# Two heads at a time in halves of the TensorE array: block-causal attention with a bilinear feed-forward, on one Trainium2 core

## The chip, the cores and the metric

The kernel runs on one core of one Trainium2 chip. Its time is the device time of one execution in microseconds (us), and the figure to be predicted is the median over several executions. Before the change three runs took 1239.2, 1240.79 and 1241.6 us, so the median is 1240.79 us.

## The reference

Eight batches of eight heads, 576 positions, 64 numbers a head. Attention is block-causal in blocks of 64 positions, and its output (4608 tokens of 512 numbers) goes into a bilinear feed-forward with 1536 hidden columns:

```python
scores = scale * np.matmul(q, k.transpose(0, 1, 3, 2))
mask = block_i >= block_j          # blocks of 64 positions
scores = np.where(mask, scores, -1000000000.0)
attn = np.exp(scores - np.max(scores, axis=-1, keepdims=True))
attn = attn / (np.sum(attn, axis=-1, keepdims=True) + 1e-09)
x = np.matmul(attn, v)             # then heads side by side: (4608, 512)
out = ((x @ w_a) * (x @ w_b)) @ w_out
```

All inputs are float32. q and k are drawn about four times larger than in the plain problem, so the scores need more than one low-precision product.

## The kernel before

Much of the kernel's arithmetic is done on float32 numbers that are split in two: a high part in the format float32r (fp32r), which TensorE takes in one pass, and the rest, the low part, also in fp32r. A plain float32 matmul is used where nothing is split; it shows in the trace as two records of one matmul.

There are three stages. The first is attention, head by head, with the first third of the feed-forward (four of the twelve blocks of 128 hidden columns, called the MoE below) filled in between. The second finishes that first third, and the third does the other eight blocks by another scheme. The change touches the first stage alone.

One head in the first stage, by the names of the code:

- `softmax` makes the scores. Positions are taken in four query tiles of 128 (t = 0 to 3, with 192, 320, 448 and 512 keys) and one "side" tile of 128 by 128 for the 64 positions that are left over at each end. TensorE (PE) writes the scores to a PSUM bank (tile `s`, or `sl` for t = 3), VectorE (DVE) sets the masked corner with a memset and takes the row maximum (`top`, a TENSOR_REDUCE to `nm`; `nb` joins the maxima of t = 3 and side), and ScalarE (ACT) computes the exponential with the sum of each row (`exps`, an ACTIVATE and a READ_ACCUMULATOR, to tile `e`). DVE makes the reciprocal `rc` of the sums, and GpSimd (POOL) multiplies `e` by it, tile by tile.
- `turn` transposes `e` on PE in blocks of 128 by 128 (fourteen for a head, into the PSUM tile `tp`, of which there are two). ACT copies `tp` to `ah` in fp32r, and DVE writes the low part to `al`.
- `values` multiplies by v. v too is split, and its high and low parts stand side by side as 128 columns (`v2`), so that one matmul gives both products; `ah` and `al` are run through it one after the other, and ACT and DVE add the two halves of the result to `xf` (`avlo`). ACT and POOL split `xf` for the MoE (`xh`, `xl`).

Scores are two fp32r products with 128 contraction rows. To that end `split_q` and `split_k` make the high and low parts for a pair of heads, and `spread` copies them by DMA, issued from SyncE's queue (SP), so that 64 rows of one head hold the high and 64 the low part of q against the same part of k. The first eight heads (`NATIVE = 8`) use plain float32 for scores and output; each then uses 64 of PE's rows for scores and 64 of its columns for the output.

The order of the work is a table, `SLOT`: for a slot s, one head long, it lists which step of which head comes next and how many units of filling follow it. `want` turns the place in the slots into a count of MoE matmuls that should have been emitted by then; they start in slot 10 (`MOE_FROM = 10.2`). `PE_ORDER` is empty, so a scheduler then settles the order of the instructions on each engine. `mm3` (line 223) makes the MoE's matmuls, twelve to a PSUM bank (tiles `ps` and `pso`), and there are two such banks: before the next but one group of twelve starts, ACT must have copied the bank out (`a`, line 247, or `ob`, line 560), or DVE must have multiplied it (`hf`, line 249). Weights arrive packed and are converted on DVE and ACT (`convert_w`) during the first ten slots.

## Time and profile before

| | before |
|---|---|
| time, median of three runs | 1240.79 us (1239.2 to 1241.6) |
| span of the profiled execution | 1238.6 us |
| PE busy, share of the span | 1222.5 us, 99% |
| DVE, ACT, POOL busy | 974.6, 706.6, 415.5 us |
| mean granted TensorE clock | 0.994 |
| first matmul of the MoE | 95.2 us |
| last matmul of `values` | 628.4 us |

The span runs from the first to the last instruction of the profiled execution; its own time is not listed apart, and the three timed runs lie 0.6 to 3.0 us above the span, their median 2.2 us. "Busy" is the time in which an engine had at least one instruction at work. Matmuls overlap one another, and so do instructions of ACT and DVE by about 0.1 us, so what an instruction costs a full queue is the distance from its start to the next one's start, not its own duration.

### The profile page before, as it was taken

The numbers are of one execution on the slowest core, as the hardware profiler recorded it, in microseconds if no ns is written. First come the engines' busy times: TensorE is split into PE (matmuls) and PEld (weight loads), VectorE is DVE, ScalarE is ACT, GpSimd is POOL, SyncE is SP. The second block draws the span as 40 slices with busy tenths as digits, with TensorE's granted clock in tenths as the row PEclk, the third lists the DMA queues.
The fourth block names the chain that finished last, engine by engine and source line by source line (L and its number), as shares of the span: only waits on it lengthen the run. The fifth ranks groups of instructions, "written<-read, shape, count | busy, mean of one in ns | idle before, by whom it ended". The sixth has DMA issues, their size and how long they took to land.

```text
span 1238.6 us, 23305 instructions
## 1 busy us (share of the span) xinstructions
PE 1222.5 (99%) x7849; PEld 1170.0 (94%) x7849; DVE 974.6 (79%) x2485; ACT 706.6 (57%) x1770; POOL 415.5 (34%) x583
## 2 busy tenths in 40 slices
PE   9989999999999999999999999999999999999998
PEld 5668999999999999999999999999999999999998
DVE  6898888777877778778889988878878677677654
ACT  5788878788788887888756345334334222222210
POOL 4467666566665666656500022022021000000000
PEclk8999999999999999999999999999999999999999
DMA  6468766767667776676234266266298344144131
GB/s 222 140 185 224 199 161 166 188 170 185 164 172 181 176 185 164 169 182 158 71 121 150 92 152 167 82 157 162 76 258 272 122 141 127 40 140 126 28 103 64
DMA packets 86583, 187.13 MB, mean 151 GB/s; under 512 B 11200, under 2 KB 46016, under 8 KB 86464
## 3 DMA queue, kind: packets, MB, share of 16 engines
q1 hardware_dynamic: 74944, 166.76, 48.6%
q0 software_dynamic: 6912, 9.44, 4.8%
q10 hardware_dynamic: 4608, 9.44, 2.2%
q8 instruction: 63, 1.03, 0.3%
q14 instruction: 56, 0.46, 0.1%
HBM read 87.03 MB, written 47.19 MB: 108 GB/s over the span
## 4 chain that ended last, share of the span: by engine, by line
PE 85%; DVE 7%; DMA 3%; ACT 2%; issue 1%; POOL 1%; SPq 0%; ACTq 0%; DVEq 0%; POOLq 0%
PE pso_z L792 15%; PE ps L223 12%; PE psx_z L746 8%; PE psw_z L746 8%; PE psv_z L746 8%; PE tp L474 8%; PE pso L223 5%; PE s L398 5%; PE psy_z L746 4%; PE av L523 3%; PE av L529 3%; PE sl L398 2%; PE av L513 2%; PE s L418 1%; DMA kp<-kT 1%
## 5 line engine op out<-in xcount | busy, mean ns | idle before, releaser
L223 PE MATMUL ps<-xh,wab 128*128 128x288 f32 x1024 | 240.7, 303 | 0.0
L792 PE MATMUL pso_z<-h_z,wo 128*128 128x384 f32 x1152 | 203.1, 334 | 0.0
L451 POOL TENSOR_SCALAR e<-e,rc 128x512 f32<-128x512 f32 (+3 forms) x256 | 154.6, 616 | 137.7 <-DVE rc L448 122.7
L792 PEld LDWEIGHTS pso_z<-h_z,wo 128*128 128x128 f32 x1152 | 199.9, 188 | 0.4 <-ACT h_z L112 0.3
L223 PEld LDWEIGHTS ps<-xh,wab 128*128 128x128 f32 x1024 | 172.0, 188 | 3.4
L223 PE MATMUL ps<-xl,wab 128*128 128x288 f32 x512 | 154.2, 301 | 0.0
L478 DVE TENSOR_TENSOR al<-tp,ah 128x512 fp32r<-128x512 f32 x224 | 131.7, 607 | 27.7 <-ACT ah L476 26.7
L112 ACT CAST h_z<-u_z 128x384 fp32r<-128x384 f32 x96 | 49.3, 514 | 180.0 <-DVE u_z L771 163.4
L476 ACT CAST ah<-tp 128x512 fp32r<-128x512 f32 x224 | 116.7, 533 | 53.0 <-PE tp L474 49.5
L474 PE MATMUL tp<-ident,e 128*128 128x128 f32 x832 | 135.9, 278 | 5.0 <-DVE al L478 1.8
L855 POOL DMA_DIRECT2D part<-pt x48 | 42.8, 1012 | 291.4 <-ACT pt L854 291.3
L474 PEld LDWEIGHTS tp<-ident,e 128*128 128x128 f32 x832 | 100.5, 141 | 20.0 <-issue 6.7
L223 PE MATMUL pso<-hh,wo 128*128 128x288 f32 x480 | 118.6, 308 | 0.0
L746 PE MATMUL psx_z<-xh,wab 128*128 128x384 f32 x384 | 116.4, 338 | 1.8 <-DVE u_z L764 1.8
L407 ACT ACTIVATE e<-s,nm 128x192 f32<-128x192 f32 (+2 forms) x192 | 101.8, 530 | 28.3 <-DVE nm L404 18.4
L746 PE MATMUL psw_z<-xh,wab 128*128 128x384 f32 x384 | 116.2, 338 | 0.0
L746 PE MATMUL psv_z<-xh,wab 128*128 128x384 f32 x384 | 116.2, 338 | 0.0
L404 DVE TENSOR_REDUCE nm<-s 128x1 f32<-128x128 f32 (+3 forms) x256 | 109.8, 430 | 2.1
L223 PEld LDWEIGHTS ps<-xl,wab 128*128 128x128 f32 x512 | 96.4, 188 | 3.6 <-POOL xl L115 0.2
L398 PE MATMUL s<-k,q 128*128 128x256 f32 x336 | 80.7, 321 | 2.1 <-ACT e_s L407 1.6
L223 PEld LDWEIGHTS pso<-hh,wo 128*128 128x128 f32 x480 | 81.5, 189 | 1.2
L115 POOL TENSOR_TENSOR v<-vr,v 128x320 fp32r<-128x320 f32 x56 | 49.7, 887 | 91.6 <-ACT v L112 78.6
(147 smaller groups left out, 2857.9 us busy)
## 6 DMA issues: line engine op xcount, KB each, us to landing
k<-kp SPq DMA_DIRECT2D x112, 288.0 KB, 4.2
xr<-xd SPq DMA_DIRECT2D x48, 384.0 KB, 4.0
q<-qp SPq DMA_DIRECT2D x112, 160.0 KB, 2.5
raww<-wab SPq DMA_DIRECT2D x24, 512.0 KB, 3.8
qp<-qT SPq DMA_DIRECT2D x32, 320.0 KB, 3.2
vr<-vm SPq DMA_DIRECT2D x64, 160.0 KB, 3.3
kp<-kT SPq DMA_DIRECT2D x32, 288.0 KB, 3.3
xd<-xf ACTq DMA_DIRECT2D x32, 288.0 KB, 4.8
```

The lines of the kernel that those rows point to most:

```text
L112: nc.scalar.copy(hi, src)
L115: return lo_eng.tensor_tensor(lo, src, f32(hi), op=ALU.subtract)
L223: mm = nc.tensor.matmul(ps, w_, d_, start=(i == 0), stop=(i == n - 1))
L398: mark = nc.tensor.matmul(ps[:, :w], qm[:, q0[t]:q0[t] + P], kk[:, :w], start=(i == 0), stop=(i == len(ks) - 1))
L404: nc.vector.tensor_reduce(nm[:, t:t + 1], view, axis=AX.X, op=ALU.max, negate=True)
L407: nc.scalar.activation(out, view, AF.Exp, bias=bias, accum_out=sm[:, t, :1])
L451: nc.gpsimd.tensor_scalar(ev, ev, rc[:, t:t + 1], 1.0, op0=ALU.mult, op1=ALU.mult)
L474: mark = nc.tensor.transpose(tp[:, c], src, ident)
L476: nc.scalar.copy(ah[:, :m, cols], tp[:, :m])
L478: return nc.vector.tensor_tensor(al[:, :m, cols], tp[:, :m], f32(ah[:, :m, cols]), op=ALU.subtract)
L746: nc.tensor.matmul(ps, wt[:, i, iw], j[:, ix], start=start and kp == 0 and i == 0 and j is xh, stop=kp == KP - 1 and i == 1, skip_group_ch ...
L792: nc.tensor.matmul(ps, wt[:, a, osl], b, start=i == 0, stop=i == 3 * len(fs) - 1)
```

## The change

The unit of the first stage becomes a pair of heads, h = 0 and 1.

- Scores (`softmax`): q and k of the pair lie under each other in 128 partitions, as they are loaded. Head 0 uses PE's rows 0 to 63 and head 1 rows 64 to 127, matmul by matmul in turn, each into a PSUM bank of its own (`ps_sc` has 4 banks, before 3). There are three fp32r products for each tile (high by high, high by low, low by high). The tiles of a pair come in two steps: t = 3, side and t = 1 in the first, t = 2 and t = 0 in the second. Narrow tiles are no longer widened to 256 columns.
- Output (`values`): plain float32 for every head. v and the transposed weights `ah` are not split: no `al`, no `split_v`, no `avlo`. Head 0 writes the columns' lower half (PSUM partitions 0 to 63) and head 1 the upper half of one tile `av`, in turn, and DVE copies the tile to `xf` in two instructions. `av` takes its bank from the two `tp` tiles.
- `spread` and its DMAs go. The split of q and k for a pair stays.
- The transposes are the same, but t = 0 of both heads shares one `tp` and one copy.
- `NATIVE = 6` now counts pairs, so twelve heads have plain float32 scores. The matmuls that kept the clock up in the first two slots (`KEEP`) go. Four buffers of `e` instead of two.
- `SLOT` is now for a pair, and `PE_ORDER = ["PE"]`: PE takes its instructions in the order in which the code emits them; the other engines are ordered by the scheduler as before.

The core of the diff:

```diff
-PE_ORDER = []
-NATIVE = 8
+PE_ORDER = ["PE"]
+KEEP = {}
+NATIVE = 6
...
-    ps_sc = psum(right, "ps_sc", 3)
+    ps_sc = psum(right, "ps_sc", 4)
...
-    def spread(i):
-    def split_v(i):
...
+    rows = slice(D), slice(D, P)
+    def products(p, x, y):
+        if p < NATIVE:
+            return [(x[:, 0], y[:, 0])]
+        x, y = x.bitcast(F32R), y.bitcast(F32R)
+        return [(x[:, 1], y[:, 1]), (x[:, 1], y[:, 0]), (x[:, 0], y[:, 1])]
...
+        def scores(t, outs):
+            for j, (qq, kk) in enumerate(qk):
+                for h, r in enumerate(rows):
+                    keys = ends(kk[r]) if t == NT else kk[r, :nk[t]]
+                    mark = nc.tensor.matmul(
+                        outs[h], qq[r, q0[t]:q0[t] + P], keys, start=j == 0, stop=j == len(qk) - 1)
...
+        def both(out, c, src, cols, start, stop):
+            for i, r in enumerate(rows):
+                mark = nc.tensor.matmul(
+                    out[r], v[:, i, c], a[:, i, src, cols], start=start, stop=stop, skip_group_check=True)
+        for c in range(NCH):
+            a0 = max(P * c - BLK, 0)
+            both(av[:, a0:], c, c, slice(a0, W), c == 0, False)
+        both(av[:, W - BLK:], NCH, SIDE, SC[1], False, True)
+        mark = both(av0, NCH, SIDE, SC[0], True, True)
+        nc.vector.tensor_copy(xf[:, BLK:], av)
+        nc.vector.tensor_copy(xf[:, :BLK], av0)
...
+    SLOT = [(V_, -2, 0), (S_, 0, 12), (T_, -1, 7), (T_, -1, 7), (T_, -1, 8), (S_, 0, 12), (T_, -1, 6),
+            (T_, -1, 6), (T_, -1, 6), (T_, -1, 8)]
```

How the change moves the instructions is seen at two places, in the middle of the stage (batch 3, head 4). The first is PE at the start of that head's scores. A row gives line, operation, output, inputs and columns. In the program before, the names are `s1` (t = 1 and side), `sl` (t = 3), `ps0` (a MoE group of twelve), `k2` and `q2` (the spread parts):

```order
L223 MATMUL pso_1_1_3_3945<-hh_1_1_3_3677,wo3_85 128x288
L418 MATMUL s13_4_3981<-k23_4_3768,q23_4_3767 128x128 x2
L398 MATMUL sl3_4_3980<-k23_4_3768,q23_4_3767 128x512 x2
L223 MATMUL ps0_2_0_1_3997<-xh2_0_0_2651,wab1_80 128x288
L223 MATMUL ps0_2_0_1_3997<-xl2_0_0_2652,wab1_80 128x288
```

The same place after the change, where `s33_4_0` and `s33_4_1` are t = 3 of the two heads and `av0` the last tile of an earlier pair's output:

```order
L471 MATMUL av03_0_3270<-ah3_0_3092,v3_0_2758 64x64 x2
L383 MATMUL s33_4_0_3300<-k3_4_2918,q3_4_2921 128x512
L383 MATMUL s33_4_1_3301<-k3_4_2918,q3_4_2921 128x512
L383 MATMUL s33_4_0_3300<-k3_4_2918,q3_4_2921 128x512
L383 MATMUL s33_4_1_3301<-k3_4_2918,q3_4_2921 128x512
L383 MATMUL s33_4_0_3300<-k3_4_2918,q3_4_2921 128x512
L383 MATMUL s33_4_1_3301<-k3_4_2918,q3_4_2921 128x512
L383 MATMUL s13_4_0_3302<-k3_4_2918,q3_4_2921 128x128
```

Two matmuls for one head between MoE matmuls became six for two heads, directly behind the output of the pair before the last; two more tiles of six follow before the next MoE matmul.

The second place is ACT, where the exponentials of that head stand among the copies out of the MoE's banks. Before (`e0_...` from `s1`, `sl`, `s0` are the head's exponentials, `a` the copy of a MoE bank, `ah` of a transposed tile):

```order
L407 ACTIVATE e0_s_115,sm0_113<-s13_4_3981,nb3_4_3979 128x128
L407 ACTIVATE e0_3_109,sm0_113<-sl3_4_3980,nb3_4_3979 128x512
L407 ACTIVATE e0_0_106,sm0_113<-s03_4_4022,nm3_4_3977 128x192
L247 COPY a_2_0_1_4039<-ps0_2_0_1_3997 128x288
L476 CAST ah3_3_4056<-tp3_3_3_4058 128x4x128
L407 ACTIVATE e0_1_107,sm0_113<-s13_4_3981,nm3_4_3977 128x320
```

After the change, from the pair's first exponential (t = 3, side, then further on t = 2 and t = 0 of both heads; `q4_0` is the high part of q of a later pair):

```order
L391 ACTIVATE e0_3_109,sm0_138<-s33_4_0_3300,nb3_4_3299 128x512
L391 ACTIVATE e1_3_117,sm0_138<-s33_4_1_3301,nb3_4_3299 128x512
L391 ACTIVATE e0_s_113,sm0_138<-s13_4_0_3302,nb3_4_3299 128x128
L391 ACTIVATE e1_s_121,sm0_138<-s13_4_1_3303,nb3_4_3299 128x128
L456 COPY ah3_2_3358<-tp3_2_3_0_3359 128x4x128
L247 COPY a_2_0_1_3365<-ps0_2_0_1_3345 128x288
```

```order
L391 ACTIVATE e0_2_108,sm0_138<-s23_4_0_3409,nm3_4_3297 128x448
L391 ACTIVATE e1_2_116,sm0_138<-s23_4_1_3410,nm3_4_3297 128x448
L348 ACTIVATE q4_0_3457<-qr4_0_3458 128x640
L391 ACTIVATE e0_0_106,sm0_138<-s03_4_0_3411,nm3_4_3297 128x192
L391 ACTIVATE e1_0_114,sm0_138<-s03_4_1_3412,nm3_4_3297 128x192
L247 COPY a_2_0_2_3462<-ps0_2_0_2_3392 128x288
L112 CAST k4_0_3454<-kr4_0_3455 128x576
```

Each copy `a` of a MoE bank now stands behind four exponentials and one more instruction, where before two or three exponentials stood between two copies.

More of the change, by code (lines that the diff above doesn't have):

```diff
@@ L283, in attention_then_bilinear_ffn @@
     NCH = (S - BLK) // P
-    c0 = [min(max(P * c - BLK, 0), S - BLK - 256) for c in range(NCH)]
     W = S - BLK
@@ L313, in attention_then_bilinear_ffn, with pair_of @@
     xs_all = {}
[L315 to L317 removed]
+    def pair_of(p):
         b, h = divmod(2 * p, H)
[L320 to L331 removed]
@@ new lines, in load_qk, with load_v, parts_of @@
+    def load_qk(p):
+        b, h, n = pair_of(p)
+        take(p, "k", S, kT[b, h:h + 2].rearrange("h d s -> (h d) s"))
+        take(p, "q", SQ, qT[b, h:h + 2].rearrange("h d s -> (h d) s"))
+    def load_v(p):
+        b, h, n = pair_of(p)
+        vv = heads[p]["v"] = apool.tile([P, 2, NCH + 1, D], F32, tag="v", name=f"v{n}", bufs=3)
+        for j in range(2):
+            nc.sync.dma_start(vv[:, j], vm[b, h + j])
+    def parts_of(p, tag):
+        return heads[p].pop(f"{tag}r"), *(heads[p][tag].bitcast(F32R)[:, j] for j in (1, 0))
@@ L663, in attention_then_bilinear_ffn @@
             due += m
-            now = s + due / fill
+            now = 2 * (s + due / fill)
             while n_conv < 5 * int(now * CONV_PER_SLOT + CONV0):
```

343 lines of the change are left out of this document (121 added, 222 removed).

## Prediction

> **What bounds the kernel now.** I read the page first, then the windows, then the order of time on PE, ACT and DVE inside one stretch of the attention stage. A change smaller than 0.2% (2.5 us) could not be told from none.
>
> From the page: the span, and the busy time of PE and of its weight loads.
>
> ```profile
> span 1238.6 us, 23305 instructions
> PE 1222.5 (99%) x7849; PEld 1170.0 (94%) x7849; DVE 974.6 (79%) x2485; ACT 706.6 (57%) x1770; POOL 415.5 (34%) x583
> ```
>
> Next the windows: length, then busy time and count by engine. The first row is the start, the second the middle of the stage. The third holds the `sl` matmuls alone (two to a head), the fourth the MoE matmuls of line 223, from head 10's scores to head 62's.
>
> ```profile
> 5.00:94.60 89.60, 83.57 (x500) 56.74 (x498) 78.01 (x225) 67.85 (x185) 47.31 (x56) 0.92 0.59 180
> 267.10:577.80 310.70, 310.30 (x2243) 298.20 (x2242) 247.03 (x785) 250.46 (x706) 191.03 (x273) 1.00 0.69 173
> 94.60:596.80 502.20, 35.17 (x104) 1.00 0.71 177
> 94.60:596.80 502.20, 337.04 (x1824) 1.00 0.71 177
> ```
>
> In the middle PE is busy 310.30 of 310.70 us: the stage is as long as PE's work, and DVE, ACT and POOL have room. 104 records are 52 heads in 502.2 us, 9.66 us a head or **19.32 us a pair**, and 1824 / 26 = 70 MoE matmuls go with each pair. So the price of the change is the difference per pair, times 26, with the start apart.
>
> What PE spends is read from starts (start, length, engine, line, matmul, count). Rows that no difference needs are left out, among them the second record of line 527 and the four of line 529 behind the first row.
>
> ```profile
> 301.71 0.22 PE L527 MATMUL av<-ah,v 128*128 128x128 f32 x1
> 302.63 0.29 PE L223 MATMUL pso<-hh,wo 128*128 128x288 f32 x1
> ...
> 303.03 0.56 PE L398 MATMUL s<-k,q 128*128 128x448 f32 x2
> 303.43 0.30 PE L223 MATMUL pso<-hh,wo 128*128 128x288 f32 x1
> ...
> 304.54 0.43 PE L223 MATMUL pso<-hh,wo 128*128 128x288 f32 x2
> 304.80 0.30 PE L223 MATMUL pso<-hl,wo 128*128 128x288 f32 x1
> 304.94 0.49 PE L474 MATMUL tp<-ident,e 128*128 128x128 f32 x3
> ...
> 305.64 0.29 PE L223 MATMUL pso<-hl,wo 128*128 128x288 f32 x1
> ...
> 305.91 0.34 PE L418 MATMUL s<-k,q 128*128 128x128 f32 x2
> 306.08 0.68 PE L398 MATMUL sl<-k,q 128*128 128x512 f32 x2
> 306.60 0.29 PE L223 MATMUL ps<-xh,wab 128*128 128x288 f32 x1
> ...
> 309.10 0.96 PE L523 MATMUL av<-ah,v 128*128 128x512 f32 x4
> 309.90 0.46 PE L398 MATMUL s<-k,q 128*128 128x320 f32 x2
> 310.19 0.43 PE L223 MATMUL ps<-xh,wab 128*128 128x288 f32 x2
> ```
>
> A MoE matmul takes (304.94 - 304.54) / 3 = 0.133 us. Between 304.94 and 305.64 lie four transposes and two MoE matmuls: (0.70 - 0.27) / 4 = 0.108 us a transpose. Score matmuls: 0.26 us for 512 columns, 0.20 for 448, 0.145 for 320, 0.085 for 128; for 256 columns I interpolate 0.12. A head's scores are twice their sum, 1.62 us; its output 0.92 + 0.80 = 1.72 us; its 14 transposes 1.51 us. A pair is then 2 x 4.85 + 70 x 0.133 = 19.0 us, near the 19.32 that the windows give.
>
> **The change, part by part.** *Row halves.* Do two heads in two halves of the rows run side by side? Before, odd and even float32 heads stand in different halves, and where they meet the trace shows it:
>
> ```profile
> 32.15 0.37 PE L418 MATMUL s<-kp,qp 64*128 64x128 f32 x1
> 32.15 0.69 PE L398 MATMUL sl<-kp,qp 64*128 64x512 f32 x1
> 32.36 0.27 PE L418 MATMUL s<-kp,qp 64*128 64x128 f32 x1
> 32.69 0.59 PE L398 MATMUL sl<-kp,qp 64*128 64x512 f32 x1
> ```
>
> Both start at 32.15. So a pair's scores cost one head's three products: 3 x (0.23 + 0.20 + 0.145 + 0.11 + 0.11) = **2.39 us** (0.23 for a second 512-column matmul, whose weights are loaded in time; 0.11 for 192 and 128 columns, a little above the measured 128). Before they cost 3.24. Without overlap they would cost 4.78.
>
> *Column halves, and the price of going from one form to another.* Float32 output with 64 columns, and what stands around it:
>
> ```profile
> 36.31 0.66 PE L474 MATMUL tp<-ident,e 128*128 128x128 f32 x4
> 36.90 1.32 PE L513 MATMUL av<-ah,vr 128*64 128x128 f32 x12
> 38.15 0.80 PE L398 MATMUL s<-kp,qp 64*128 64x320 f32 x2
> 38.88 0.45 PE L513 MATMUL av<-ah,vr 128*64 128x64 f32 x4
> ```
>
> Four transposes take 0.59 us to the next start instead of 0.43, so 0.15 us goes into the new form. The next twelve records (eight of 128 columns and four of 64, 1280 columns) take 1.25 us, 1.10 without such a step: 0.86 ns a column and record, two records a matmul. The 320 columns take 0.73 us, 0.19 more than 2 x 320 x 0.86 ns. So each change of form costs 0.15 to 0.2 us, and before there are none in the middle of the stage, where all rows say 128*128.
> Now one head's output is 512 + 448 + 320 + 192 + 64 + 64 = 1600 columns, 2.75 us in float32. If the two heads overlap, a pair costs **2.75 us**, against 3.44 before; if not, 5.50. No row of before has two column halves at work, so both ends stay in the range; I take 2.75, since row halves, the nearest rows, overlap fully. The Trainium skill ("TensorEngine Tiling (Array Packing)", Key Properties) says that different tiles load and multiply in parallel, which no run here shows for columns.
>
> There are five changes of form a pair (into the output, from it to the scores, out of the scores, and once more into and out): 0.9 us. The three DMA queues and POOL lose work or keep it (no `spread`, no `v` split; POOL scales q of the float32 pairs, which DVE did), and PE waited for none of it. DVE loses `al` and `avlo`, ACT `avlo`: they were hidden behind PE and gain nothing by themselves.
>
> PE's work is 70 x 0.133 + 28 x 0.108 + 2.39 + 2.75 + 0.9 = **18.4 us**, 0.9 below 19.32.
>
> *New waits.* PE now keeps to the written order, and there are two MoE banks. PE can't begin the next but one group of twelve before ACT has copied the bank. Ahead of these copies stand now the exponentials of a pair. ACT's starts, DVE's maxima, and the mean of a 448-column maximum by form:
>
> ```profile
> 302.63 0.74 ACT L343 ACTIVATE qp<-qp 128x640 fp32r<-128x640 f32 x1
> 303.27 0.57 ACT L536 COPY avlo<-av 64x512 f32<-64x512 f32 x1
> ...
> 305.76 0.64 ACT L407 ACTIVATE e<-s,nm 128x448 f32<-128x448 f32 x1
> ...
> 306.39 1.07 ACT L476 CAST ah<-tp 128x512 fp32r<-128x512 f32 x2
> 307.33 0.42 ACT L560 COPY ob<-pso 128x288 f32<-128x288 f32 x1
> ...
> 308.94 0.37 ACT L407 ACTIVATE e_s<-s,nb 128x128 f32<-128x128 f32 x1
> ...
> 309.30 0.69 ACT L407 ACTIVATE e<-sl,nb 128x512 f32<-128x512 f32 x1
> ...
> 309.96 0.43 ACT L407 ACTIVATE e<-s,nm 128x192 f32<-128x192 f32 x1
> ...
> 310.36 0.41 ACT L247 COPY a<-ps 128x288 f32<-128x288 f32 x1
> ```
>
> ```profile
> 306.79 0.69 DVE L404 TENSOR_REDUCE nm<-sl 128x1 f32<-128x512 f32 x1 [0.15 <-PE sl L398]
> ...
> 308.00 0.28 DVE L404 TENSOR_REDUCE nm<-s 128x1 f32<-128x128 f32 x1
> ```
>
> ```profile
> L404 DVE TENSOR_REDUCE nm<-s 128x1 f32<-128x448 f32 x64 | 39.2, 613 | 0.6
> ```
>
> By starts an exponential with its sum takes 0.36 us (128 columns), 0.40 (192), 0.63 (448), 0.66 (512); a copy to `ah` 0.47; q's high part 0.64.
> The second step of the scores: from the start of the last t = 2 product it ends after about 0.4; a memset (put at 0.1) and the first maximum (0.61) bring it to 1.1; then 2 x 0.63 + 0.64 + 2 x 0.40 on ACT and 0.41 for the copy: done at 4.2. PE in the meantime does 0.20 + 3 x 0.11 (t = 0), 0.2 (form), 12 matmuls, four transposes and 2 more matmuls: 0.73 + 14 x 0.133 + 0.43 = 3.0. **It waits 1.2 us.**
> The first step: end of t = 3 at 0.4, two maxima 1.3 (0.69 the second, a little less the first), four memsets and the side's two maxima 0.9 (0.28 a maximum; the memsets are my estimate), `nb` 0.3 (an estimate too, two tiny instructions): 2.9; then 2 x 0.66 + 2 x 0.36 + 0.47 + 0.41 = 2.9: copied at 5.8. PE: 0.23 + 3 x (0.11 + 0.145) + 0.2 + 24 x 0.133 + 8 x 0.108 = 5.3. **It waits 0.5 us.**
>
> A pair takes 18.4 + 1.7 = 20.1 us, 0.8 more than 19.32; 26 pairs make **+21 us**. These chains are the weakest terms; each may be 0.5 us off, and so the sum 26 us either way.
>
> *The start.* Until 94.6 us DVE is busy 78.0 of 89.6 us (scores and weights), and the change leaves both there. Less PE work can gain 12 us at most; but within a slot output, scores and transposes now follow one another in written order, two heads at a time, with DVE between them. I take nothing, with 10 us each way. What follows attention is unchanged.
>
> Sum against the profiled execution: 1238.6 + 21 = 1260 us of span. The median lies 2.2 us above it, hence **1262 us**.
>
> **The rivals.**
> 1. *The waits don't come*: if ACT is ahead of these sums, PE's 18.4 us stand alone, 26 x 0.9 = 23 us less: 1217 us. For it: ACT is busy 250 of 311 us, with less to do afterwards. Against: what counts is not its load but what stands ahead of the copy. It decides from waits under 0.9 us a pair.
> 2. *Both effects cancel*: 1240 us.
> 3. *Halves overlap in part*, say three quarters of the saving: (2.39 + 2.75) / 4 = 1.3 us a pair more, 1296 us. Against: the second `sl` record above starts 0.54 us after the first; 512 x 0.86 ns is 0.44, and the rest a change of form, so nothing is lost there. The Trainium skill ("TensorE: Matmul & The Clock Gate", Part 3: Packing small matmuls) reports 2.38 times for three column tiles and 3.07 for four row tiles, 0.79 and 0.77 of the ideal; an estimate by that page is 1.4 us a pair more, 1299 us.
> 4. *Column halves don't overlap*: 2.75 us a pair more, 1262 + 72 = 1334 us. For it: nothing shows that they do.
> 5. *Row halves don't overlap in fp32r* (the rows above are float32): 2.4 us more, less the first wait, which PE would then fill: 1.9 x 26 = 49, 1311 us.
>
> **How the numbers follow.** My forecast has a chance of 0.45 (1236 to 1288 us by the chains and the start), the first rival 0.30, the second 0.06, the third 0.07, the fourth 0.09, the fifth 0.03. The range goes from 1204 (most of the first rival, with some gain at the start) to 1308; outside stay the fourth and fifth and what is left of the first, 0.19 in all. Faster 0.30, no change 0.06, slower 0.64.
>
> **What would show it.** Score records of one pair in `64*128` with two starts within 0.02 us, and `128*64` records of `av` likewise, would show the overlap; 19.3 or 20.1 us between the scores of neighbouring pairs decides between first rival and forecast; PE's idle time in front of line 223, put down to ACT's `a` and `ob`, should be 1.7 us a pair. I am wrong if that idle time is under 0.9 us, or if the pair's output takes 5.5 us.

## The result: slower by 4.7%

The changed kernel takes 1298.70 us (1296.1 to 1300.42, four runs) against 1241.19 us (1239.2 to 1242.09) for the kernel before beside it: 1.0469 times as long, 95% interval 1.0447 to 1.0490, or 57.5 us more. The forecast was 1262 us: the sign is right, the size is not.

### The profile page after: what moved, and what is told of

It is laid out like the page before. It is cut to its first block, busy times and chain, and to the rows that moved or that the text cites. A ratio compares the mean times of both kernels' runs of the same rounds, so it can differ in the third digit from the quotient of the medians.

```text
span 1298.6 us, 22050 instructions
## 1 busy us (share of the span) xinstructions
PE 1208.5 (93%) x8045; PEld 1098.4 (85%) x8045; DVE 790.7 (61%) x1932; ACT 620.6 (48%) x1550; POOL 351.9 (27%) x540
## 4 chain that ended last, share of the span: by engine, by line
PE 74%; DVE 11%; ACT 11%; issue 3%; DMA 1%; SPq 0%; ACTq 0%; DVEq 0%
PE pso_z L722 14%; PE ps L223 9%; PE psw_z L676 7%; PE psx_z L676 7%; PE av L471 7%; PE pso L223 7%; PE psv_z L676 7%; PE s L383 6%; ACT e L391 6%; PE tp L453 5%; DVE nm L388 4%; PE psy_z L676 3%; ACT ah L456 2%; ACT e_s L391 1%; ACT a L247 1%
## 5 line engine op out<-in xcount | busy, mean ns | idle before, releaser
L223 PE MATMUL ps<-xh,wab 128*128 128x288 f32 x1024 | 230.4, 304 | 18.0 <-ACT a L247 18.0
L434 POOL TENSOR_SCALAR e<-e,rc 128x512 f32<-128x512 f32 (+3 forms) x256 | 149.2, 602 | 129.5 <-DVE rc L430 127.8
L456 ACT COPY ah<-tp 128x512 f32<-128x512 f32 x224 | 134.3, 604 | 40.0 <-PE tp L453 40.0
L388 DVE TENSOR_REDUCE nm<-s 128x1 f32<-128x512 f32 (+4 forms) x320 | 146.8, 484 | 10.3 <-PE s L383 6.3
L383 PE MATMUL s<-k,q 64*128 64x512 f32 (+3 forms) x900 | 113.1, 369 | 26.2 <-ACT e L391 25.8
L223 PE MATMUL pso<-hh,wo 128*128 128x288 f32 x480 | 106.1, 302 | 20.9 <-ACT ob L502 13.0
L383 PEld LDWEIGHTS s<-k,q 64*128 64x128 f32 x900 | 78.7, 193 | 52.4 <-ACT e L391 37.2
L453 PEld LDWEIGHTS tp<-ident,e 128*128 128x128 f32 x832 | 105.3, 146 | 18.7 <-issue 8.9
L391 ACT ACTIVATE e<-s,nm 128x448 f32<-128x448 f32 (+2 forms) x192 | 102.5, 540 | 38.2 <-DVE nm L388 37.9
L480 DVE COPY xf<-av 128x512 f32<-128x512 f32 x32 | 22.1, 691 | 138.7 <-PE av L471 138.1
L471 PE MATMUL av<-ah,v 128*64 128x64 f32 (+4 forms) x768 | 99.4, 410 | 3.0 <-ACT ah L456 3.0
```

The lines of the kernel that those rows point to most:

```text
L223: mm = nc.tensor.matmul(ps, w_, d_, start=(i == 0), stop=(i == n - 1))
L383: mark = nc.tensor.matmul(outs[h], qq[r, q0[t]:q0[t] + P], keys, start=j == 0, stop=j == len(qk) - 1)
L388: nc.vector.tensor_reduce(nm[:, h, t:t + 1], view, axis=AX.X, op=ALU.max, negate=True)
L391: nc.scalar.activation(out, view, AF.Exp, bias=bias, accum_out=sm[:, h, t, :1])
L434: nc.gpsimd.tensor_scalar(ev, ev, rc[:, h, t:t + 1], 1.0, op0=ALU.mult, op1=ALU.mult)
L453: mark = nc.tensor.transpose(tp[:, c], src, ident)
```

## The profile after

First the page of the changed kernel: the span, and the busy time of PE and the other engines.

```profile
span 1298.6 us, 22050 instructions
PE 1208.5 (93%) x8045; PEld 1098.4 (85%) x8045; DVE 790.7 (61%) x1932; ACT 620.6 (48%) x1550; POOL 351.9 (27%) x540
```

Every engine has less to do than before, PE by 14 us, and still the span is 60 us longer: PE now waits. Where it waits, the windows say (length, busy time and count by engine, granted clock, DMA share, GB/s): the start up to the first MoE matmul, nine pairs in the middle, all from the first MoE matmul to the first of stage 3, and stage 3.

```profile
5.00:114.90 109.90, 75.98 (x322) 42.43 (x320) 79.66 (x208) 60.69 (x162) 46.16 (x64) 0.66 0.41 130
311.51:500.30 188.79, 172.59 (x1389) 148.88 (x1388) 80.25 (x270) 115.81 (x333) 87.42 (x138) 1.00 0.25 75
114.90:728.20 613.30, 569.16 (x4550) 496.60 (x4549) 280.75 (x901) 374.90 (x1057) 260.72 (x408) 1.00 0.25 76
728.20:1298.60 570.40, 559.80 (x3170) 556.54 (x3169) 429.76 (x825) 183.57 (x331) 42.60 (x48) 0.99 0.46 130
```

The last two stretches of the kernel before, by the same marks (its first MoE matmul starts at 95.2 us):

```profile
94.60:677.00 582.40, 579.21 (x4177) 555.63 (x4176) 474.27 (x1459) 455.81 (x1258) 324.07 (x465) 1.00 0.66 167
677.00:1238.60 561.60, 556.22 (x3170) 554.77 (x3168) 421.61 (x803) 181.47 (x327) 42.77 (x48) 1.00 0.45 129
```

By the exact starts (first MoE matmul 114.92 us, before 95.23; first matmul of stage 3 at 728.27, before 677.04) the 60.0 us fall into three parts: **19.7 in the start**, 613.35 - 581.81 = **31.5 from there to stage 3**, and 570.3 - 561.6 = **8.7 in stage 3**.

Next, one pair on PE in order of time (start, length, matmul, count, and in brackets the idle time before it with what ended it). The last two rows are the output's first matmuls one pair and nine pairs later.

```profile
311.51 2.92 PE L471 MATMUL av<-ah,v 128*64 128x512 f32 x24
314.37 1.74 PE L383 MATMUL s<-k,q 64*128 64x512 f32 x18
...
320.07 0.29 PE L223 MATMUL ps<-xh,wab 128*128 128x288 f32 x1
321.00 0.40 PE L223 MATMUL pso<-hh,wo 128*128 128x288 f32 x1 [0.65 <-ACT a L247]
...
322.95 1.18 PE L383 MATMUL s<-k,q 64*128 64x448 f32 x12
...
326.31 0.30 PE L223 MATMUL pso<-hh,wo 128*128 128x288 f32 x1
327.81 0.40 PE L223 MATMUL pso<-hh,wo 128*128 128x288 f32 x1 [1.21 <-ACT ob L502]
...
332.49 0.65 PE L471 MATMUL av<-ah,v 128*64 128x512 f32 x2
...
500.26 0.65 PE L471 MATMUL av<-ah,v 128*64 128x512 f32 x2
```

The pair's output takes 314.37 - 311.51 = 2.86 us, its two score steps 1.67 and 1.11 us (to the next matmul), changes of form included: both kinds of halves overlap fully. A pair takes (500.26 - 311.51) / 9 = 20.97 us. Twice PE stops for a MoE bank: the starts lie 0.93 and 1.50 us apart where neighbours lie 0.13 apart. With the slower first matmul after each stop (the next one starts 0.24 us later, not 0.13) that is 0.9 + 1.5 = 2.4 us a pair. The profile's own account of PE's waits in the nine pairs (us, times, longest) counts only the idle time and has 16.2 us, 1.8 a pair, all of it for the copies `a` and `ob`:

```profile
PE ps L223 <- ACT a L247: 7.0, 8, 1.2
PE pso L223 <- ACT ob L502: 6.0, 5, 1.2
PE pso L223 <- ACT a L247: 3.2, 5, 0.7
```

ACT and DVE show why:

```profile
318.03 0.69 ACT L391 ACTIVATE e<-s,nb 128x512 f32<-128x512 f32 x1 [2.04 <-DVE nb L412]
...
319.71 0.37 ACT L391 ACTIVATE e_s<-s,nb 128x128 f32<-128x128 f32 x1
...
320.52 0.43 ACT L247 COPY a<-ps 128x288 f32<-128x288 f32 x1
...
324.70 0.63 ACT L391 ACTIVATE e<-s,nm 128x448 f32<-128x448 f32 x1 [1.43 <-DVE nm L388]
...
325.94 0.73 ACT L348 ACTIVATE q<-qr 128x640 fp32r<-128x640 f32 x1
...
326.96 0.42 ACT L391 ACTIVATE e<-s,nm 128x192 f32<-128x192 f32 x1
...
327.35 0.41 ACT L502 COPY ob<-pso 128x288 f32<-128x288 f32 x1
```

```profile
314.37 0.69 DVE L480 COPY xf<-av 128x512 f32<-128x512 f32 x1 [2.23 <-PE av L471]
...
315.37 1.29 DVE L388 TENSOR_REDUCE nm<-s 128x1 f32<-128x512 f32 x2 [0.18 <-PE s L383]
...
319.90 0.11 DVE L395 MEMSET s<- 64x64 f32 x1 [1.97 <-ACT e_s L391]
```

The two copies stand behind four exponentials and a copy `ah`, and behind five activations, as the prediction had it, and its chains were only a little short. They count from the start of the last t = 3 product, which the trace has at 314.94 us: the first maximum starts 0.43 us later (forecast 0.4), the exponentials 3.1 us later (2.9), and the copy `a` ends 6.0 us later (5.8). PE comes to the matmul that needs the bank after 5.3 us, as forecast. In the second step `ob` ends 4.3 us behind the start of the last t = 2 product (4.2). DVE's copy of the output, which stands ahead of the maxima, doesn't delay them: DVE waits for the scores behind it. The last row shows DVE idle for 1.97 us: the memset of the t = 1 tile waits for ACT's exponentials of the side block, whose columns lie in the same bank.

In the start PE waits for something else. The largest row of PE's waits up to the first MoE matmul, changed kernel first and then the kernel before (us, times, longest):

```profile
PE s L383 <- ACT e L391: 25.1, 10, 11.6
```

```profile
PE s L398 <- ACT e_s L407: 2.4, 3, 1.3
```

Both score steps of a pair use all four score banks, so the second step waits until the first step's exponentials have emptied them, and there is no MoE work yet to put beside it. The longest wait is the first pair's, and DVE's first instructions tell its cause: the weights' first conversion waits for its DMA, and the first maximum stands behind it (in e2 below, without that, it runs at 7.34 us).

```profile
9.66 0.43 DVE L141 TENSOR_SCALAR sw<-raww 128x512 int32<-128x512 int32 x1 [8.26 <-DMA raww<-wab]
...
12.85 0.68 DVE L388 TENSOR_REDUCE nm<-s 128x1 f32<-128x512 f32 x1
```

In the first 35 us of stage 3 PE waits, longest (2.1 and 1.6 us) for DVE's tile `u_z`. These 35 us, changed kernel first and then the kernel before: DVE is as busy, but PE gets through 155 matmuls instead of 197, and the granted clock is 0.90 instead of 1.00.

```profile
728.20:763.20 35.00, 30.45 (x155) 28.53 (x155) 33.84 (x75) 14.37 (x27) 0.00 (x0) 0.90 0.43 137
```

```profile
677.00:712.00 35.00, 34.16 (x197) 33.84 (x196) 33.99 (x71) 15.15 (x29) 0.00 (x0) 1.00 0.35 110
```

By counts of starts the loss appears between the 80th and the 140th matmul of the stage (the 80th starts 0.7 us earlier after the stage's first than before the change, the 140th 7.1 us later, the last 8.7 us later); DVE converts weights in that time. How much of the loss is the wait and how much the clock behind it isn't separated. When the last transpose of attention starts, 1959 of the 2256 MoE matmuls of line 223 have started, and 1919 before: 40 fewer are left to convert beside.

How the loss builds up, counted from the starts in four traces. A cell gives the start of the last transpose of that pair and, by then, the MoE matmuls started; "lag" is the difference to the kernel before, less 0.133 us for each MoE matmul in hand. The last two columns belong to experiments below (e1 and c4).

| pair | before | changed | lag | e1, lag | c4, lag |
|---|---|---|---|---|---|
| 1 | 33.4 / 0 | 43.3 / 0 | 9.9 | 9.8 | 3.5 |
| 4 | 86.2 / 0 | 106.8 / 0 | 20.6 | 19.6 | 4.9 |
| 6 | 124.0 / 88 | 146.6 / 110 | 19.7 | 18.6 | 4.7 |
| 9 | 180.1 / 278 | 205.8 / 304 | 22.2 | 19.5 | 4.2 |
| 20 | 394.4 / 1071 | 436.1 / 1096 | 38.4 | 19.4 | -2.3 |
| 30 | 588.4 / 1791 | 644.3 / 1816 | 52.6 | 19.4 | -7.8 |

Half of the start's loss is there after the first pair, all of it after the fourth. From the ninth pair on 1.5 us come with every pair.

## The experiments

The theory (A): the loss has three places, the MoE banks whose copies stand behind exponentials in ACT's program, the start's score banks with the first conversion ahead of the first maximum, and stage 3's late weights. Rivals: B, the pair is bound by its own round from scores to exponentials, or by DVE; C, the low granted clock costs the start; D, a gain in the start is given back, because the weight conversions bound it; E, the halves' order in PE's program doesn't matter. All kernels start from the changed one. The times are medians, the ratios are to the kernel before in the same comparison.

### The waits at the MoE banks

**e1**: `a` and `ob` are copied by DVE.

```diff
-nc.scalar.copy(a_sb, ps[:, :n])
+nc.vector.tensor_copy(a_sb, ps[:, :n])
...
-nc.scalar.copy(ob, ps)
+nc.vector.tensor_copy(ob, ps)
```

> The copies a and ob, which empty the MoE banks, are on DVE instead of ACT. Theory A (of the 57.5 us lost, the larger part are two waits of PE in each pair for a MoE bank whose copy stands behind exponentials in ACT's queue, 0.9 and 1.47 us where the pair's length is 20.97): the idle time ahead of the MoE matmuls falls from 39 us to under 8, neighbouring pairs lie 18.6 to 18.9 us apart, the time is 1242 to 1256 us. Rival B (the pair's length is set by the round from scores through maxima and exponentials back to the score banks, or by DVE once it has the copies too): the wait moves to the scores, pairs stay 20.2 us or more apart, the time is 1280 to 1299 us.

Measured: 1268.41 us, ratio 1.022 (1.0195 to 1.0246), 30 us less than the change. All waits of PE in ten pairs (301.55 to 496.1 us, 19.45 us each):

```profile
PE tp L453 <- ACT ah L456: 4.0, 18, 0.3
```

No wait for a MoE bank is left, and that is worth 30 us, net of the waits that took their place. For 19.45 us a pair is not 18.6: transposes now wait for their two banks, whose copies `ah` stand behind the same exponentials. Neither A nor B had the number, and A's place was right.

**e9** was meant for stage 3: `behind = 3 * F1 * NO + 40` leaves 40 more MoE matmuls behind attention.

> 40 MoE matmuls fewer are put beside attention and 40 more are left behind it, as many as before the change. Theory A (stage 3 lasts 8.7 us longer because DVE has 40 matmuls less time to convert the next weights in, so that PE waits between the 80th and the 140th matmul of the stage): the stage lasts 561 to 564 us instead of 570.3, the attention ends some 5 us earlier and the stretch behind it is 5 us longer, the time is 1290 to 1294 us. Rival (DVE's order in that stretch and not its length): 1297 to 1300 us.

Measured: 1273.82 us, ratio 1.0274 (1.0256 to 1.0291). Stage 3 takes 565.7 us, 4.6 less; but most of the gain of 25 us is elsewhere: pairs lie 19.8 us apart (300.0 to 498.1 us, ten pairs), although copies and engines are untouched. PE's waits in that stretch, and two rows of ACT in one pair:

```profile
PE tp L453 <- ACT ah L456: 5.0, 15, 0.6
PE ps L223 <- ACT ob L502: 1.0, 5, 0.2
```

```profile
404.67 0.40 ACT L502 COPY ob<-pso 128x288 f32<-128x288 f32 x1 [0.94 <-PE pso L223]
405.78 0.69 ACT L391 ACTIVATE e<-s,nb 128x512 f32<-128x512 f32 x1 [0.71 <-DVE nb L412]
```

A bank takes 12 matmuls and a pair 72, so the banks end at the same places in every pair. In the changed kernel one ends with the 12th matmul behind the first score step, just as the exponentials begin (318.03 us above), and its copy comes behind them at 320.52, although ACT had been idle for 2.04 us. 40 matmuls later in the count a bank ends with the fourth, and its copy fits into that idle time. Two runs test this reading; the expectations speak of 24 matmuls a bank, which is the pair of banks that one block of hidden columns takes. 48 keeps the phase by either count.

**e11** and **e12**: 48 and 32 instead of 40.

> 48 MoE matmuls, twice a bank's 24, are put behind attention instead of 40. Phase theory (what took 1.2 us a pair off with 40 was that the bank changes fell elsewhere in the pair, 40 being 16 more than 24): the pairs lie 20.9 to 21.0 us apart again, only stage 3 gains its 4.6 us or a little more, the time is 1291 to 1296 us. Rival (fewer MoE matmuls beside attention help by themselves): 19.7 to 19.9 us, 1270 to 1276 us.

> 32 MoE matmuls behind attention: the bank changes come 8 matmuls later in the pair than in the changed kernel. Phase theory: the distance between pairs differs from both 20.97 and 19.79 us, anywhere from 19.2 to 21.5 us, and the waits stand at other MoE runs than the two of the changed kernel. Rival (fewer MoE matmuls beside attention help by themselves): 19.7 to 20.0 us and 1273 to 1278 us, with the waits at the same places.

Measured: e11 1298.82 us (1.0469, 1.0436 to 1.0501) with pairs 20.97 us apart again; e12, one run, 1289.34 us with pairs 20.4 us apart, and its waits at other places (from 306 to 493 us 7.1 us ahead of transposes and 2.6 ahead of MoE matmuls). The phase decides, not the amount. And e11 gained nothing although its stage 3 takes only 564.4 us: the 48 matmuls (6.4 us) went from a stretch that waits anyway to one in which PE has to do them.

### The start

**e2**: `CONV0 = 0`, and each step of a conversion is ordered behind the latest pair's `rc` on DVE.

```diff
-            if paced:
-                behind_of(ins, "hf")
+            behind_of(ins, "hf" if paced else "rc")
```

> The first weight conversion stands behind the first pair's softmax on DVE, and each later one behind the latest pair's rc. Theory A (the start's 19.7 us are lost before the first transpose, at 31.1 us where it was 16.3 us, most of it because the first maximum stands behind a conversion that waits for the weights): the first maximum runs at about 7 us where it was 12.9, the first transpose at 24 to 26 us, the first MoE matmul at 107 to 110 us where it was 114.9, the time is 1290 to 1294 us. Rival C (the low granted clock of the start, 0.50 to 0.84, costs it): the first transpose comes at 29 us or later, the time is 1297 to 1300 us. Rival D (a conversion that starts later keeps the first MoE matmul where it is): the first transpose comes earlier and the first MoE matmul does not.

Measured: 1299.51 us (1.0469, 1.0445 to 1.0493). The first maximum runs at 7.34 us instead of 12.85:

```profile
7.34 1.29 DVE L386 TENSOR_REDUCE nm<-s 128x1 f32<-128x512 f32 x2 [5.93 <-PE s L381]
```

The first transpose starts at 21.05 us instead of 31.06 and the first MoE matmul at 108.7 instead of 114.9; the sixth pair ends at 146.1 us instead of 146.6. A's cause is right for the first pair. The total went as D says, gained and given back before the sixth pair, but D's reason isn't shown. From the first MoE matmul to the sixth pair's end DVE is busy 26.1 us (16.0 in the change), PE waits 3.2 us there for one `ah`, and behind that wait the granted clock is 0.58 for four us (136.6 to 140.6), where the change has 1.00 in these pairs.

**e3**: 108 matmuls of zeros (`KEEP`), into an idle MoE bank, in the first five pairs.

> Matmuls of zeros into an unused MoE bank stand in the first five pairs' program on PE, 106 in all, to keep the clock granted. Rival C (the low clock costs the start): granted clock 0.9 to 1.0 from 20 to 120 us, the first MoE matmul 8 to 11 us earlier than 114.9 us, the time 1288 to 1291 us. Theory A (the first pair's wait for DVE costs it, and from the first av matmul on the two kernels need the same 70.4 us to the first MoE matmul, although the clocks differ): the clock rises, the first MoE matmul comes 0 to 4 us earlier, the time is 1295 to 1300 us.

Measured: 1299.42 us (1.0466, 1.0438 to 1.0494). The granted clock up to the first MoE matmul rises from 0.66 to 0.87, and that matmul starts at 113.4 us, 1.5 earlier. But the zeros are work too: PE is busy 88.7 us up to there, against 76.0, so this run alone can't price the clock. What speaks against C as the main cost is c4 below, whose first MoE matmul starts 18.2 us earlier than the change's at a granted clock of 0.70.

**e8**: in the first five pairs the t = 2 scores use the two MoE banks, which are idle then.

```diff
-            return [ps_sc.tile([P, 512], F32, tag="sc", name=f"s{t}{n}_{h}") for h in range(2)]
+            pl, tag = (ps_mm, "mm") if t == 2 and p < 5 else (ps_sc, "sc")
+            return [pl.tile([P, 512], F32, tag=tag, name=f"s{t}{n}_{h}") for h in range(2)]
```

> In the first five pairs, before any MoE matmul, the second step's larger tile uses the two idle MoE banks for its scores. Theory A (the start is lost because both score steps share four banks, so that the second step's scores wait for the first step's exponentials, 25 us in the first 108 us): that wait falls under 12 us, the first MoE matmul comes at 103 to 108 us instead of 114.9, and the gain is kept: 1287 to 1293 us. Rival D (the start is bounded by the weight conversions on DVE and by the pairs' own chains, as in the run where the conversions came later): the first MoE matmul comes earlier by less than 3 us or the gain is given back by pair 5, 1296 to 1300 us.

Measured: 1294.91 us (1.0466, 1.0437 to 1.0495, so not told apart from the change). PE's two largest waits up to 104.2 us:

```profile
PE tp L454 <- ACT ah L457: 15.8, 9, 3.8
PE s L384 <- ACT e L392: 11.6, 3, 10.8
```

The score banks' waits are gone but for the first pair's, and a wait of the transposes has taken their place. Still the first MoE matmul starts at 104.3 us, 10.6 earlier; at the sixth pair's end 6.1 us of it are left. The stretch between the two, e8 first and then the change:

```profile
104.20:140.50 36.30, 33.43 (x230) 28.28 (x229) 18.41 (x61) 24.20 (x69) 15.73 (x22) 0.91 0.29 93
114.90:146.60 31.70, 29.44 (x231) 25.42 (x229) 15.95 (x58) 23.43 (x68) 13.78 (x21) 1.00 0.23 69
```

With the same matmuls PE is busy 4.0 us longer, at a lower clock: 0.50 from 112.2 to 116.2 us and 0.68 in the next four, right behind a wait for score banks. So most of what is given back here goes with the clock. No run holds the clock in that place.

**e6**: the maxima of the t = 1 tile come before the side block's exponentials, so that DVE does not wait for ACT (`[0]` stands for memset and maximum, `[1]` for the exponential).

```diff
+        masked(1, ps[1], [0])
         for h in range(2):
             exps(LAST, h, eb[h][0][LAST], ps[LAST][h], nb[:, h, :1])
...
-        masked(1, ps[1])
+        masked(1, ps[1], [1])
```

> Only the order of the softmax is changed: the maxima of the tile that shares its bank with the side block come before the exponentials of that block, so that DVE does not wait for ACT in the first step (it waited 1.5 to 2 us there in each pair). Theory A (the start is the round from scores through maxima and exponentials back to the four score banks): PE's wait for score banks before 107 us falls from 25 us to 13 to 18 us, the 28 transposes of the fourth pair end at 97 to 101 us instead of 106.8, and 7 to 10 us of it are kept to the sixth pair. In the steady stretch all six exponentials now stand in one piece ahead of the copy a, so the first step's wait for a MoE bank grows from 0.9 to 1.2 to 1.8 us and takes 5 to 15 us back: 1290 to 1303 us. Rival (the start is bounded by the weight conversions): the sixth pair ends within 3 us of where it did, 1297 to 1312 us.

Measured: 1324.52 us (1.0686, 1.0669 to 1.0703), 26 us more than the change. The start did as A has it (fourth pair 6.5 us earlier, though only 2.9 of them are left at the sixth). The rest is the other side: six exponentials now stand in one piece ahead of `a`, and pairs lie 22.06 us apart. PE's waits in nine pairs:

```profile
PE ps L223 <- ACT a L247: 14.2, 10, 1.7
PE pso L223 <- ACT a L247: 6.9, 4, 1.7
PE pso L223 <- ACT ob L506: 4.8, 4, 1.2
```

A shorter chain for the scores is a longer one for the copies behind it; I had priced that at 5 to 15 us, and it was about 28 (from the sixth pair's end to the last one's 560.4 us, in the change 532.8).

### Stage 3

**e7**: `STEP = 680` instead of 800, so the conversions behind attention come faster.

> The weight conversions after attention come every 680 instead of every 800 units of MoE work. Theory A (the 8.7 us lost in stage 3 are PE's wait for weights there, because 40 MoE matmuls fewer are left after attention to convert beside): stage 3 lasts 563 to 567 us instead of 570.3, the time is 1290 to 1296 us. Rival (DVE has no room for them there): 1297 to 1301 us.

Measured: 1296.34 us (1.0463, 1.0447 to 1.0478). Stage 3 takes 568.4 us, 1.9 less, and the total is not told apart from the change. That is little: in runs that leave this stage as it is it takes from 569.0 (e8) to 572.2 us (e3). At the stage's 140th matmul the loss has fallen from 7.1 to 2.4 us, but at the 400th it is 6.7 (8.1 in the change), so it moved more than it went. Only e9 (565.7 us) and e11 (564.4 us) lie clearly below: the stage is shorter when more MoE matmuls are left in front of it. That DVE's time for the conversions is the reason is argued and not shown, and in e11 the total gained nothing by it.

### The halves

**e5**: all of the first head's output products, then all of the second's. **e10**: three of one, three of the other. **e4**: scores of a tile, three products of one head, then three of the other. The edit of e4:

```diff
-            for j, (qq, kk) in enumerate(qk):
-                for h, r in enumerate(rows):
+            for h, r in enumerate(rows):
+                for j, (qq, kk) in enumerate(qk):
```

> In the output all 12 products of the first head are issued, then all 12 of the second, instead of in turns. If two column halves run beside each other only when neighbours in PE's order (theory A, which reads 2.86 us for the 24 records as full overlap): the 24 records take 5.4 to 5.7 us, a pair 2.6 us more, the time is 1298.7 + 2.6 x 30 = 1365 to 1385 us. Rival E (PE lets the second head's records run ahead of the first's by themselves): 2.9 us for the 24 records, 1297 to 1302 us.

> The output's products are issued three of the first head, three of the second, and so on. The row halves of the scores ran beside each other although three products of one head stood ahead of the other's. If the column halves do so too (PE lets a free half run ahead over a few instructions): the 24 records take 2.9 to 3.2 us, 1297 to 1305 us. If they run beside each other only as direct neighbours: in each group one of three overlaps at the seam, the 24 records take 4.4 to 5.4 us, pairs 22.4 to 23.5 us apart, 1345 to 1379 us.

> In each tile of the scores all products of the first head are issued, then all of the second, instead of in turns. Theory A (two row halves run beside each other only as neighbours in PE's order, as the output's column halves did): the first step's 18 records take 1.67 + 1.3 = about 3.0 us, the second's 12 take 1.11 + 0.9 = about 2.0 us, neighbouring pairs lie 22.9 to 23.2 us apart, the time is 1345 to 1365 us. Rival (the later score banks give the waits at the MoE banks more time, so part of the cost is given back): 22.0 to 22.8 us apart, 1325 to 1345 us.

(A head's output is six products of two records each, twelve records.) Measured, one run each: 1379.12, 1326.09 and 1296.26 us. The output's row in e5, in e10, and the two score steps' rows in e4:

```profile
412.13 5.45 PE L480 MATMUL av<-ah,v 128*64 128x512 f32 x24
```

```profile
407.44 3.83 PE L481 MATMUL av<-ah,v 128*64 128x512 f32 x24
```

```profile
313.76 1.74 PE L383 MATMUL s<-k,q 64*128 64x512 f32 x18
...
322.61 1.18 PE L383 MATMUL s<-k,q 64*128 64x448 f32 x12
```

One after the other costs the output 2.5 us a pair and the kernel 80 us, so the overlap of the column halves is worth that. In e4 nothing is lost: the two heads' records start in pairs, 0.01 us apart, though three products of one stand ahead. For e4 and e10 the expectations were wrong; the last section has the rule that fits the three.

### The parts joined

**c1**: e1 and e6, and two of a pair's seven copies `ah` (the first and the fourth) on DVE.

```diff
-            nc.scalar.copy(ah[(slice(None), *at)], got)
+            (nc.vector.tensor_copy if k in (0, 3) else nc.scalar.copy)(ah[(slice(None), *at)], got)
```

> The copies a and ob are on DVE, two of the seven copies ah of a pair too, and the maxima of the tile that shares its bank with the side block come before the exponentials of that block. Theory A (with the MoE banks' waits gone, what is left above PE's own work, 19.46 against 18.6 to 18.8 us a pair, is the wait of transposes for banks whose copy ah stands behind exponentials): pairs 18.6 to 18.9 us apart, the first MoE matmul 2 to 6 us earlier than 113.9, the time 1244 to 1254 us. Rival B (DVE's own queue becomes the wait): 19.4 us or more, 1266 to 1275 us.

Measured: 1246.19 us (1.0058, 1.0043 to 1.0073): 52.5 us less than the change, with pairs 18.9 us apart and no wait of PE in the trace from 300 to 497 us. A holds in the steady stretch.

**c2**: c1, `a` and `ob` on ACT again once attention is over, the conversions behind `nb` (the first one behind the first pair's), and e9's 40 matmuls. **c3**: the same with 48. **c4**: with none. **c5**: with 24. **c6**: c4 with 50 matmuls of zeros in the start.

> All that helped, together: copies a and ob and two of seven ah on DVE while attention runs, maxima ahead of the side block's exponentials, the weight conversions behind the first pair's maxima, 40 MoE matmuls more left behind attention. Theory A (the loss consists of the three places: 1.6 us a pair at MoE banks, 20 us in the start, 9 us in stage 3): the first MoE matmul at 100 to 104 us, pairs 18.7 to 18.9 us apart, stage 3 561 to 564 us long, the time 1228 to 1238 us, less than before the change. Rival (what is won at one place is waited for at the next, as in the two runs whose gain in the start was given back): 1240 to 1248 us.

> As the kernel with all that helped, with 48 instead of 40 MoE matmuls behind attention. Phase theory: pairs 18.8 to 18.9 us apart as in the kernel with copies on both engines and without the shift, where 40 gave 19.36; first MoE matmul near 98 us, stage 3 near 565 us, the time 1229 to 1236 us, less than before the change. Rival: pairs 19.3 us or more, 1244 to 1252 us.

> The kernel with all parts, without the 48 MoE matmuls left behind attention. If the moved work costs where it goes what stage 3 gains (the stretch in which MoE ramps up waits for its pairs and not for the number of matmuls): stage 3 568 to 571 us instead of 565, the last transpose and the last MoE matmul as many us earlier, the time 1237 to 1242 us as with 48. If moving them was a gain: 1243 to 1248 us.

> 24 MoE matmuls left behind attention, the same phase. By either reading between its neighbours, 1237 to 1245 us; pairs 18.8 to 18.9 us apart.

> As the kernel with all parts and nothing moved behind attention, with 50 matmuls of zeros in the first five pairs. If the clock granted to the start costs nothing once the waits are gone: within 2 us of that kernel. If it does: granted clock 0.9 and more from 20 us on, the first MoE matmul 3 to 6 us earlier, 1233 to 1238 us.

| | time, us | ratio, interval | first MoE matmul | us a pair | stage 3, us |
|---|---|---|---|---|---|
| c1 | 1246.19 | 1.0058, 1.0043 to 1.0073 | 105.9 | 18.88 | 570.9 |
| c2 | 1251.94 | 1.0100, 1.0082 to 1.0117 | 97.9 | 19.37 | 564.7 |
| c3 | 1240.33 | 0.9997, 0.9980 to 1.0013 | 96.3 | 18.87 | 565.3 |
| c4 | 1238.47 | 0.9996, 0.9984 to 1.0008 | 96.7 | 18.91 | 571.5 |
| c5 | 1238.12 | 0.9990, 0.9978 to 1.0002 | 97.9 | 19.16 | 564.8 |
| c6 | 1239.93 | 0.9990, 0.9969 to 1.0011 | 98.4 | 18.91 | 568.7 |

The phase of the MoE banks shows again in c2 against c3: from 300 to 500 us PE waits 1.9 us for `a` and `ob` in c2 and for nothing in c3. c5's 19.16 us a pair say nothing about the phase. Its traced execution has a granted clock of 0.95 from the first MoE matmul on, where c3 and c4 have 1.00, PE waits for nothing from 300 to 500 us, and the same matmuls take longer; so whether 24 keeps the phase stays open. c2 and c3 were expected to come out faster than the kernel before, and neither did. c3, c4 and c5 are the same within the intervals: what stage 3 gains by matmuls left behind attention, they cost there. c6 has a granted clock of 0.89 in the start instead of 0.70 and gains nothing by its zeros; its first MoE matmul starts 1.7 us later than c4's. No version was found that beats the kernel before by a measurable amount; the best ones win back all that the change lost. The stretches of c4 by the marks used above, and ten pairs:

```profile
5.00:96.60 91.60, 69.84 (x322) 41.26 (x320) 78.46 (x206) 53.74 (x150) 42.06 (x55) 0.70 0.42 139
96.60:667.80 571.20, 562.78 (x4550) 495.04 (x4549) 356.90 (x1078) 314.10 (x894) 267.28 (x417) 1.00 0.27 84
667.80:1239.40 571.60, 561.60 (x3170) 558.41 (x3168) 429.72 (x825) 183.73 (x330) 42.63 (x48) 0.99 0.45 129
301.80:490.80 189.00, 188.78 (x1541) 164.46 (x1540) 113.85 (x360) 106.04 (x310) 96.23 (x151) 1.00 0.27 83
```

Against the kernel before c4 has 1.5 us more in the start, 10.7 us less between (571.2 against 581.8), and 10 us more in stage 3.

## Why the prediction was partly right and mostly too small

- **The halves: right.** Forecast 2.75 us for a pair's output and 2.39 for its scores, plus 0.9 for changes of form; measured 2.86 and 2.78 with most of those changes in them. Rivals 3, 4 and 5 fall. By the Trainium skill ("TensorEngine Tiling (Array Packing)", Key Properties) different tiles load weights and multiply in parallel; the trace now agrees for column halves, with both heads in 2.86 us where e5 shows 5.38 one after the other. The 0.79 of the ideal that I drew from the Trainium skill ("TensorE: Matmul & The Clock Gate", Part 3) for rival 3 did not come. That rival 3's time, 1296 us, lies next to the measured 1298.70 is an accident: its mechanism is absent.
- **PE's work, 18.4 us a pair: nearly right.** It counted 70 MoE matmuls; a pair in the middle has 72, which makes it 18.7. c4, where PE is busy 188.78 of 189.0 us, takes 18.9.
- **The new waits: the right place and cause, the size too small.** Forecast 0.5 and 1.2 us, measured 0.9 and 1.5. The two chains came out 0.2 and 0.1 us longer than their sums, 0.13 us of it in `nb`, which I had estimated. The rest is PE's restart, which the sum left out: 0.05 us from the copy's end to PE's next start, and 0.24 us instead of 0.13 to the one after it, twice a pair. By the prediction's own sign, idle time ahead of line 223, it is 1.8 us a pair against 1.7, and the output took 2.86 us and not 5.5: neither sign of being wrong came, because both watch the middle of the stage, and the larger part of the error lies outside it. 20.1 us a pair were forecast, 20.97 measured; from the first MoE matmul to stage 3 that made 31.5 us instead of 21. e1 shows the cause, and e9 with e11 shows that the size hangs on where in the pair a bank happens to end, which the sum took as given and did not name.
- **"I take nothing" for the start: the step that failed most.** Measured 19.7 us. The prediction looked at DVE's load, which the change leaves, and not at the chain: four banks for two steps that need four each, two heads instead of one before the first transpose can run, a conversion ahead of the first maximum. e2, e8 and e6 each shorten it, and c4 starts its MoE 18 us earlier. Alone e2, e6 and e8 lost between two fifths of it and all of it again before the sixth pair. Why is shown only in part: in e8 4.0 us of it are the same matmuls at a lower granted clock, in e2 3.2 us are a wait for `ah`.
- **"What follows attention is unchanged": wrong by 8.7 us.** The code is unchanged, but it depends on how much MoE work is left as cover when attention ends, and that fell by 40 matmuls. e9 and e11 took 4.6 and 5.9 us off the stage by leaving more; the rest of the loss stays open.

The sum, by spans: 21 forecast, plus 10.5 from the first MoE matmul to stage 3 (longer waits and two more MoE matmuls a pair), 19.7 in the start and 8.7 in stage 3, makes 59.9 of the 60.0 us. The first rival (no waits, 1217 us) had the mechanism of c4 but not its price: with the waits gone, start and stage 3 eat the 0.4 us a pair that the halves save (10.7 us over some 26 pairs).

## What to carry to other kernels

When the unit of work is doubled, the saving per unit is the easy part; ask what the first unit, which has no neighbour to hide behind, now waits for, and what later stage used the work that has moved as cover. When the order on the bounding engine is fixed by hand and filler work runs through it in a fixed rhythm, look where in the unit each filler buffer ends: a copy that becomes ready together with a block of long instructions on its engine waits for the whole block, in every unit, and a shift of a few instructions decides about more than 1 us a unit. And an order that shortens one chain through an in-order engine lengthens the ones behind it (e6): move the copies to another engine first.

## What the hardware showed that was not expected

- A record of one half of the array can start up to four places ahead of its turn, if its half is free. In e5 the second head's first record (the thirteenth) starts at 414.660 us, 6 ns behind the ninth (414.654) and ahead of the tenth (414.71); in e10 the seventh starts with the third (408.358 and 408.352); in e4 the fourth starts 0.01 us behind the first. So turns of one to three records cost little or nothing (e4), of six cost 0.9 us a pair (e10), of twelve 2.5 us. The Trainium skill ("TensorE: Matmul & The Clock Gate", Part 3, The mechanism) says that matmuls start strictly in program order; these starts differ, and the measurement decides.
- In e8 a wait of PE was followed by a lower granted clock. PE is busy 2.7 of the 4 us up to 112.2 us; in the next four the clock is 0.50, in the four after them 0.68, with PE busy throughout, and 230 matmuls took 4.0 us more than in the change.
- Matmuls of zeros raised the granted clock of the start (from 0.66 to 0.87 in e3, from 0.70 to 0.89 in c6 against c4) and brought nothing to the total; the first MoE matmul came 1.5 us earlier in e3 and 1.7 us later in c6, since the zeros take PE's time.
- The first MoE matmul behind a wait is followed by the next one after 0.24 us instead of 0.13 (321.00 to 321.24 us). The same shows without a wait behind another kind of matmul (316.03 to 316.27 us, behind scores).
